# Linear attention and a routed expert layer on one core: the attention steps in another written order, with other tables of PSUM banks

## The chip, the cores and the metric

The kernel runs on one NeuronCore of a Trainium2 chip. Times are device microseconds of that core from launch to end; a kernel's time is the median of its runs. Lower is better. Five engines work side by side and each takes its own instructions strictly in order: TensorE (PE; its weight loads are PEld), VectorE (DVE), ScalarE (ACT), GpSimd (POOL) and the DMA-issuing queue of SyncE (SP).

## What is computed

```python
def phi(x):                                   # q, k, v: 8 batches, 8 heads, 576 tokens, 64 wide
    proj = einsum('bhsd,df->bhsf', x, w_phi)  # 128 features
    proj = proj - max(abs(proj), axis=-1)
    return concat([exp(proj), exp(-proj)])    # 256 features
kv  = einsum('bhsf,bhsd->bhfd', phi(k), v);   z = sum(phi(k), axis=2)
att = einsum('bhsf,bhfd->bhsd', phi(q), kv) / (einsum('bhsf,bhf->bhs', phi(q), z) + 1e-6)
x   = att as 4608 rows of 512
logits = x @ w_gate + modality_bias[modality_id];  e = argmax(logits);  gate = softmax(logits)[e]
out = gate * (relu(x @ w1[e]) @ w2[e])        # 8 experts, 512 -> 1024 -> 512
```

## The kernel before

Attention comes first. Its 64 (batch, head) pairs are worked in 16 groups of four, numbered 0 to 15. Each group is a set of small generators, one per kind of work, and every generator is cut into numbered steps; `K0.9` with step 2 is written K0.9.2 here. One step mostly holds work for one engine:

- K0, K1 (`k`, L469): 1 PE projects a half of the keys (16 matmul instructions, tile `pk`, one of the two large PSUM pairs); 2 DVE takes the largest absolute value (L480); 3 DVE subtracts it (L483), which is the last reader of the PSUM pair; 4 ACT makes both exponentials (L487).
- E (`e`, L490): 1 PE projects the last 64 tokens of keys and queries into two small banks; 2 ACT copies; 3 DVE maxima (L508); 4 ACT exponentials.
- Q0, Q1 (`q`, L517): 1 PE projects queries (`pq`); 2 ACT copies them to `d` (L527); 3 POOL finds the largest absolute value over the partitions (two PARTITION_ALL_REDUCE, L531); 4 DVE subtracts (L533); 5 ACT exponentials.
- V (`v`, L541): 1 and 2 PE multiply values with the features of K0 and of K1 (32 matmul instructions each, `kvT`), 3 PE adds the last tokens, 4 ACT copies.
- T (`t`, L564): 1 PE transposes the product, 2 ACT copies. Z (`z`, L591): 1 to 3 DVE add key features in place (L598), 4 PE sums them (`zp`), 5 ACT copies, 6 PE transposes, 7 DVE copies.
- N0, N1, D, L: numerators and denominators (`pn`, `pd`, `pl`), with copies out by ACT or DVE (for D of an odd group, the second step is the DVE operation at L652). XR, XA, XB, XL: transposes back to rows (`rp`, `xp`, `rl`), scaling on DVE (L693 to L708) and the store of the rows. R: the routing of two batches, with scatters by POOL. P: the early plan of which expert rows come first, ten steps of small DVE operations (L225 to L333). ML, RL: loads of row lists and expert weights.

At the end of attention the steps of the first expert slot are mixed in: W0 to W7 split weights, TU and TV transpose gathered rows, XS and XV split those (L856, L858), M0 to M3 are the first expert matmuls (L875), S0 and S1 the second (L892). After that the remaining expert slots run one behind the other.

The order of all 889 steps is written out by hand in `ORDER` (L1154), and inside `manual_schedule` every engine of SP, PE, ACT and DVE takes its instructions in just that order. POOL's reductions are chained in the same order (`Line`). PSUM has eight banks: the pool `pm` has four small ones and `pw` has two pairs. Which one a step's tile takes is read, one entry for each tile in order, from `PM_BANKS` (158 entries) and `PW_BANKS` (118 entries) at L1198. A step that takes a bank waits until the last reader of that bank's previous tile is done. When the last K, Q or E step has been written, `pw` is closed and its room goes to the experts (L1348); transposes after that use the whole array and a `pm` bank instead of two row halves and a `pw` pair.

Of the kernel before, what the change touches and what calls it, by code (L numbers as in the profile page):

```python
# [1151 lines left out]


ORDER = """  # L1154
    K0.0 E.0 Q1.0 E.0 K0.0 K0.0 K1.0 K0.0 E.0 V.0 Q1.0 K0.1 K1.0 K1.0 K0.1 Q0.0 E.0 K1.0 K0.1 Q0.0 K0.1 V.0 V.0 V.0
# [4 lines left out]
    Z.2 E.3 E.3 Q0.3 Q1.3 Q0.3 D.1 E.3 L.1 L.1 T.2 T.2 Z.2 L.1 D.1 K0.4 K1.4 K1.3 K0.4 K1.4 K0.4 Z.2 Q1.3 N0.2 E.3  # L1160
    Q1.3 K0.4 N1.2 K1.4 V.3 Z.2 N0.2 Z.2 Z.2 E.4 N1.2 Q0.3 Q0.3 XR.1 XB.1 XR.1 XB.1 V.3 V.3 XB.1 Q1.3 Z.3 Z.3 K1.4
    Q1.4 V.3 Z.3 Q0.3 E.4 E.4 Q1.4 Q0.4 Q0.4 D.2 D.2 L.2 T.3 T.3 CB.0 E.4 K0.5 K0.5 XA.1 XA.1 L.2 K0.5 Z.3 XA.1 V.4
    K1.5 K0.5 N1.3 L.2 V.4 Q1.4 Q1.4 V.4 Q0.4 K1.5 Z.3 K1.5 Q0.4 Q1.4 Z.3 Z.3 Q1.5 V.4 E.5 Q0.5 N1.3 L.3 Q0.4 D.3 E.5
    Z.4 Q0.5 Z.4 L.3 Q1.5 T.4 Z.4 K1.5 Q0.5 L.3 K0.6 N0.3 CB.0 T.4 D.3 N0.3 Z.4 Z.4 K0.6 E.5 K0.6 K0.6 N1.4 Q0.5 Z.4
    Z.4 K1.6 K1.6 N1.4 Q0.5 Q1.5 Q1.5 E.5 XL.3 XL.3 XL.3 V.5 Q1.5 V.5 V.5 XR.3 E.6 E.6 K1.6 XR.3 V.5 K0.7 E.6 K1.6 E.6
    K0.7 Z.5 XA.3 V.6 V.6 XA.3 XA.3 L.4 D.4 K0.7 Z.5 T.5 T.5 Q1.6 Q1.6 Q1.6 Q0.6 Q0.6 Z.5 V.6 K1.7 D.4 V.6 Z.6 Z.6
    XB.3 Z.5 N0.4 K1.7 L.4 L.4 K0.7 N0.4 Z.6 K1.7 N1.5 Z.5 Q1.6 N1.5 K1.7 N0.5 XB.3 XB.3 N0.5 Z.6 Z.6 R.3 Z.5 Z.5 Q0.6
    Q1.6 Q0.6 E.7 K0.8 K0.8 Z.6 Q0.6 E.7 Z.6 K0.8 E.7 E.7 V.7 V.7 Q1.7 Q1.7 Q0.7 Z.7 Q1.7 V.7 V.7 Z.7 Q0.7 L.5 T.6 L.5
    Z.7 T.6 K0.8 K1.8 T.7 L.5 Z.7 K1.8 T.7 Q0.7 Z.7 D.5 K1.8 K1.8 Q1.7 Q1.7 D.6 D.6 D.5 N1.6 Q0.7 N0.6 Z.7 N0.6 N1.6
    Z.7 XR.5 E.8 Q0.7 Q1.8 E.8 R.3 XR.5 R.3 Q1.8 K0.9 K0.9 E.8 E.8 K0.9 V.8 V.8 XA.5 XA.5 Q0.8 L.6 Q0.8 Z.8 XA.5 V.8  # L1170
    Q1.8 K0.9 Q1.8 XB.5 L.6 L.6 Q1.8 V.8 K1.9 N0.7 XB.5 K1.9 Q0.8 Q0.8 N0.7 N1.7 D.7 XB.5 N1.7 T.8 K1.9 Q0.8 E.9 Q0.9
    E.9 Z.8 T.8 E.9 Q0.9 Q0.9 R.3 E.9 K0.10 Z.8 K1.9 Q1.9 Q1.9 Z.8 Q1.9 L.7 R.3 K0.10 K0.10 D.7 N1.8 Z.8 Z.8 Z.8 K1.10
    L.7 L.7 XL.7 V.9 R.3 K0.10 R.3 Q0.9 K1.10 V.9 Q0.9 K1.10 K1.10 XL.7 XL.7 N0.8 Q1.9 N0.8 XR.7 XA.7 XR.7 XA.7 XA.7
    V.9 V.9 Z.9 Z.9 R.7 N1.8 D.8 T.9 E.10 T.9 D.8 Q1.9 E.10 K0.11 K0.11 E.10 Q0.10 Q0.10 R.7 Z.9 V.10 V.10 K0.11 E.10
    R.7 Z.9 V.10 K0.11 V.10 K1.11 K1.11 K1.11 Q1.10 Q1.10 L.8 N1.9 Q0.10 Q0.10 K1.11 Z.9 XB.7 XB.7 XB.7 Q1.10 Q0.10
    R.7 R.7 R.7 L.8 R.7 N0.9 T.10 N1.9 N0.9 T.10 Q1.10 Q1.10 L.8 Z.10 Z.10 Q0.11 E.11 E.11 Q0.11 Q0.11 V.11 E.11 V.11
    Z.9 Z.9 K0.12 Z.10 K0.12 Q1.11 E.11 V.11 V.11 CB.0 Z.10 K0.12 L.9 Z.10 Z.10 Q1.11 Z.10 Q1.11 K1.12 T.11 R.3 D.9
    L.9 L.9 K1.12 N1.10 K0.12 Q0.11 N1.10 T.11 K1.12 D.10 D.9 Q1.11 CB.0 R.3 XR.9 XR.9 Q0.11 XA.9 XA.9 Q1.11 N0.10
    E.12 XA.9 Z.11 N0.10 Q1.12 Q0.12 E.12 Q1.12 Z.11 Q0.12 E.12 E.12 Q1.12 L.10 D.10 XB.9 K0.13 L.10 N0.11 Q0.12 R.7
    K1.12 Z.11 Z.11 Z.11 XB.9 XB.9 N0.11 N1.11 K0.13 K0.13 R.7 R.7 Q1.12 Z.11 K1.13 N1.11 K1.13 V.12 V.12 L.10 K0.13  # L1180
    Z.11 Q1.12 L.11 K1.13 L.11 D.11 Q0.12 Z.12 Z.12 Q0.12 D.11 V.12 L.11 Z.12 Q0.13 E.13 XR.11 XR.11 V.12 E.13 Q0.13
    E.13 Q0.13 Z.12 K1.13 XL.11 E.13 XL.11 R.11 Q1.13 V.13 V.13 Q1.13 XA.11 XL.11 T.12 Q1.13 R.11 R.11 R.11 Q0.13
    XA.11 Z.12 V.13 T.12 V.13 XA.11 R.11 Z.12 N0.12 N1.12 Q0.13 N0.12 Z.12 Q1.14 R.11 R.11 Q1.13 Q0.14 E.14 Q1.13 E.14
    Q0.14 Q1.14 Q0.14 D.12 P.11 D.12 N1.12 P.11 P.11 Z.13 Z.13 Z.13 K0.14 K0.14 T.13 Q1.14 R.3 Z.13 Z.13 R.11 T.13
# [5 lines left out]
    T.15 Z.15 T.15 ML.11 ML.11 W1.15 TU.15 Z.15 W3.15 Z.15 W0.15 N1.15 W3.15 N1.15 W0.15 D.15 XS.15 XS.15 XS.15 XS.15  # L1190
    L.14 D.15 L.15 L.14 L.15 L.15 W4.15 W4.15 M1.15 M1.15 M1.15 W6.15 XL.15 W5.15 XR.15 XR.15 XL.15 R.15 W5.15 R.15
    TV.15 M0.15 R.15 M3.15 W7.15 M0.15 M0.15 M3.15 R.15 N0.14 M2.15 R.15 R.15 XV.15 R.15 W6.15 M3.15 M2.15 W7.15 N0.15
    XV.15 M2.15 X3.15 X3.15 R.15 R.15 R.15 XV.15 N0.15 XV.15 S0.15 S0.15 S1.15 S1.15 XL.15 XL.15 X0.15 X0.15 X1.15
    X1.15 X2.15 X2.15
# [237 lines left out]
```

## Time and profile before

| | us |
|---|---|
| median of 3 runs | 750.12 (749.88 to 751.48) |
| the profiled execution's own time | 751.13 |
| its span, first to last instruction | 749.2 |
| PE busy in the span | 726.9 |
| attention with its handover, up to the first expert matmul | about 290 |
| only experts, 290 to 700 | PE busy 408.9 of 410 |

The page's first part gives each engine's busy time, its table in 40 slices shows where that time lies, and the table by stretches repeats it for chosen windows together with the clock that TensorE was granted (1.00 is 2.4 GHz, 0.50 is 1.2 GHz). In the lists of instructions a row that ends in `[x <-engine tile]` says that the engine stood idle for x us before it, and what ended that.

### The profile page before, as it was taken

To read this page: it belongs to the slowest core of one execution; us is meant where nothing else is said; L and a number is where in the kernel's file an instruction comes from. 1 tells how busy PE (TensorE), PEld (TensorE's weight loads), DVE (VectorE), ACT (ScalarE), POOL (GpSimd) and SP (SyncE) were. 2 spreads that over 40 slices of the span, in tenths; PEclk is the share of its full clock that TensorE was granted. 3 is DMA by queue.
4 is the path that set the end of the run, shared out by engine and by line. 5 is a ranking of instruction groups with operands and counts; after the bars stand their busy time and mean duration, and the time that the engine had idled before them with its cause. 6 is when DMAs were issued, how large, how long until landed. Compare 5 with 4: busy or idle time off the path is not lost. (4 is left out here: it accounts for less than half of the span.)

```text
span 749.2 us, 19074 instructions
## 1 busy us (share of the span) xinstructions
PE 726.9 (97%) x7617; PEld 565.4 (75%) x7617; DVE 551.3 (74%) x832; ACT 446.9 (60%) x677; POOL 298.1 (40%) x200
## 2 busy tenths in 40 slices
...
GB/s 228 192 151 169 191 107 139 72 195 160 139 123 172 34 171 299 143 292 299 279 147 391 299 349 183 294 259 225 340 280 233 366 153 208 384 295 243 210 186 31
DMA packets 57111, 161.68 MB, mean 216 GB/s; under 512 B 21481, under 2 KB 24237, under 8 KB 44720
## 3 DMA queue, kind: packets, MB, share of 16 engines
...
q8 instruction: 65, 1.06, 0.6%
...
## 5 line engine op out<-in xcount | busy, mean ns | idle before, releaser
L838 ACT CAST h<-raw 128x1024 fp32r<-128x1024 f32 x148 | 149.7, 1050 | 99.5 <-PE p L892 47.9
L840 DVE TENSOR_TENSOR l<-raw,h 128x1024 fp32r<-128x1024 f32 x148 | 175.7, 1221 | 44.2 <-ACT h L838 31.3
L531 POOL PARTITION_ALL_REDUCE mq<-d x64 | 144.3, 2321 | 85.3 <-ACT d L527 50.0
L875 PE MATMUL p<-xh,h 128*128 128x256 f32 x576 | 164.2, 285 | 0.0
L875 PE MATMUL p<-xh,l 128*128 128x256 f32 x576 | 163.4, 284 | 0.0
L875 PE MATMUL p<-xl,h 128*128 128x256 f32 x576 | 163.2, 283 | 0.0
L796 POOL DMA_INDIRECT xg<-x,me x40 | 55.2, 1380 | 175.9 <-PE pt L848 86.4
L875 PEld LDWEIGHTS p<-xh,l 128*128 128x128 f32 x576 | 110.4, 192 | 2.0 <-issue 2.0
L875 PEld LDWEIGHTS p<-xh,h 128*128 128x128 f32 x576 | 110.4, 192 | 1.6 <-issue 1.2
L875 PEld LDWEIGHTS p<-xl,h 128*128 128x128 f32 x576 | 110.4, 192 | 0.5
L881 DVE SCALAR_TENSOR_TENSOR hl<-p,hh 128x512 fp32r<-128x512 f32 x72 | 49.5, 688 | 82.9 <-ACT hh L879 82.2
L879 ACT ACTIVATE hh<-p 128x512 fp32r<-128x512 f32 x72 | 42.8, 595 | 110.6 <-PE p L875 108.3
L892 PE MATMUL p<-h,hh 128*128 128x512 f32 x272 | 104.6, 395 | 0.0
L892 PE MATMUL p<-h,hl 128*128 128x512 f32 x272 | 103.4, 390 | 0.0
L892 PE MATMUL p<-l,hh 128*128 128x512 f32 x272 | 103.2, 390 | 0.0
L538 ACT ACTIVATE qp<-d 128x1152 f32<-128x1152 f32 x64 | 70.9, 1164 | 6.8 <-DVE d L533 6.6
...
L487 ACT ACTIVATE kp<-dk 128x1024 f32<-128x1024 f32 x64 | 64.4, 1060 | 10.4 <-DVE dk L483 9.0
L598 DVE TENSOR_TENSOR kp<-kp 128x1024 f32<-128x1024 f32 x48 | 62.9, 1335 | 0.2
L550 PE MATMUL kvT<-kp,va 128*32 128x256 f32 x1024 | 59.7, 381 | 0.9 <-ACT kp L487 0.8
L892 PEld LDWEIGHTS p<-h,hl 128*128 128x128 f32 x272 | 51.1, 188 | 10.9
L892 PEld LDWEIGHTS p<-l,hh 128*128 128x128 f32 x272 | 51.1, 188 | 10.3
...
## 6 DMA issues: line engine op xcount, KB each, us to landing
...
```

The costliest lines, as they stand in the source:

```text
L487: nc.scalar.activation(kp[:, :, :, s, :].rearrange("p t a f -> p a t f"), dk, AF.Exp, scale=sc)
L531: self.line(nc.gpsimd.partition_all_reduce(mq[:, a], d[:, a], P, bass_isa.ReduceOp.absmax))
L538: nc.scalar.activation(q["qp"][:, 2 * pr:2 * pr + 2, i, :], d, AF.Exp, scale=sc)
L550: nc.tensor.matmul(pt[pr][32 * c:32 * c + 32], va[:, pr, t, 32 * c:32 * c + 32], kp[:, pr * 4 + t, c // 2, :, :], start=t == 0, stop=False ...
L598: nc.vector.tensor_tensor(kv4[:, :, t], kv4[:, :, t], kv4[:, :, u], ALU.add)
L796: g = self.nc.gpsimd.indirect_dma_start(xg, None, self.x[:rows, :], IndirectOffsetOnAxis(ix.bitcast(U32), 0), bounds_check=rows - 1, oob_i ...
L838: nc.scalar.copy(h, r)
L840: nc.vector.tensor_tensor(l, r, h, ALU.subtract)
L875: nc.tensor.matmul(pp[:, j], a[:, cc, f], b[:, cc], start=i == 0, stop=i == 11)
L879: nc.scalar.activation(self.HH[:, sl], pp, AF.Relu)
L881: nc.vector.scalar_tensor_tensor(self.HL[:, sl], pp, 0.0, self.HH[:, sl], ALU.max, ALU.subtract)
L892: nc.tensor.matmul(pp, a[:, f, tk], b[:, f], start=i == 0, stop=i == 23)
```

## The change

`ORDER` is replaced by another order of the same 889 steps: every step occurs as often as before, and only the sequence differs. `PM_BANKS` and `PW_BANKS` are replaced too, with the same number of entries. Two conditions are added so that group 15's two attention transposes (T.15 and Z.15.6) take a `pm` bank and the whole array even where they stand before the end of `pw`, as T.15 does in the new order; before, they stood behind it and did so anyway. No instruction is added, removed or resized, on any engine.

```diff
     def turns_of(self, pm, name, n, blocks):
 
-        if self.pw:
+        if self.pw and not name.endswith(str(NQ - 1)):
...
-        if self.pw:
+        if self.pw and qi < NQ - 1:
             tp = self.turns_of(pm, f"zt{n}", 1, [zT])[:, :, 0]
         else:
             tp = pz[:, P:2 * P]
...
 ORDER = """
-    K0.0 E.0 Q1.0 E.0 K0.0 K0.0 K1.0 K0.0 E.0 V.0 Q1.0 K0.1 K1.0 K1.0 K0.1 Q0.0 E.0 K1.0 K0.1 Q0.0 K0.1 V.0 V.0 V.0
-    Q1.0 Q1.0 Q1.0 Q0.0 K1.1 E.1 K0.2 K1.1 K1.1 K1.1 Q1.1 Q0.0 Q0.0 E.1 Q1.1 Z.0 Z.0 Z.0 E.1 V.1 CB.0 K0.2 V.1 Q0.1
...
-    L.12 Q0.14 Q0.14 K0.15 XB.11 XB.11 E.15 V.14 V.14 V.14 K0.15 Q1.15 Q1.14 Q1.14 P.11 N1.13 Z.14 Z.14 N1.13 L.13
-    D.13 K0.15 E.15 Q1.15 T.14 Q1.15 P.11 P.11 P.11 RL0.15 L.13 T.14 Z.14 K1.15 D.13 Q0.15 N1.14 E.15 ML.11 ML.11 L.13
-    K0.15 K1.15 K1.15 Z.14 Q0.15 XR.13 XR.13 XA.13 XA.13 XA.13 E.15 K1.15 V.15 V.15 V.15 Z.14 Q1.15 Q1.15 XB.13 Q0.15
...
+    K0.0 E.0 E.0 K0.0 K0.0 Q1.0 Q1.0 K0.0 Q0.0 Q0.0 E.0 E.0 K1.0 K1.0 K1.0 K0.1 K0.1 K1.0 Q1.0 Q1.0 Q1.0 CB.0 K0.1
+    K0.1 K1.1 K1.1 V.0 V.0 Q1.1 E.1 V.0 Z.0 V.0 V.1 Q0.0 Q0.0 Q0.0 Z.0 K1.1 K0.2 Z.0 K0.2 E.1 Q1.1 CB.0 E.1 Z.0 K1.1
...
+    E.14 Q1.14 Z.13 Z.13 V.14 P.11 Z.13 K1.14 K1.14 CB.0 K0.15 Z.13 K1.14 Q1.14 T.13 D.12 D.13 V.14 Q0.14 K0.15 Q0.14
+    K0.15 D.13 V.14 T.13 K0.15 Q0.15 P.11 V.14 Q1.14 Z.14 P.11 P.11 P.11 P.11 Q1.14 E.15 E.15 Q1.15 N0.13 Z.14 Z.14
+    N1.13 N0.13 Q1.15 N1.13 R.11 R.11 L.13 Q0.15 R.11 E.15 E.15 Q1.15 P.11 P.11 T.14 T.14 K1.15 K1.15 Z.14 V.15 K1.15
+    N1.14 RL0.15 L.13 L.13 Z.14 Z.14 ML.11 K1.15 Q1.15 Q1.15 ML.11 XR.13 V.15 Z.14 XR.13 V.15 N1.14 Q0.15 Q0.15 XA.13
...
```

## Rows read from the trace of the kernel before

**Rows 1.** The page: the span, and busy time of each engine.

```profile
span 749.2 us, 19074 instructions
PE 726.9 (97%) x7617; PEld 565.4 (75%) x7617; DVE 551.3 (74%) x832; ACT 446.9 (60%) x677; POOL 298.1 (40%) x200
```

**Rows 2.** Stretches: window, length, busy PE, PEld, DVE, ACT, POOL; clock, DMA share, GB/s.

```profile
0.00:40.00 40.00, 34.10 (x431) 20.02 (x435) 33.80 (x63) 28.77 (x49) 20.45 (x18) 1.00 0.72 197
40.00:260.00 220.00, 216.92 (x3574) 126.17 (x3566) 202.82 (x306) 184.56 (x318) 146.81 (x76) 1.00 0.49 140
269.00:272.50 3.50, 3.50 (x48) 1.93 (x36) 2.41 (x3) 2.02 (x6) 3.50 (x2) 0.51 1.01 421
290.00:700.00 410.00, 408.88 (x2917) 367.64 (x2910) 264.60 (x400) 193.65 (x252) 103.36 (x87) 1.00 0.73 271
```

**Rows 3.** Instructions of PE in order: start, us, line, tile, count [idle before].

```profile
23.03 1.13 PE L523 MATMUL pq<-qt,wp 64*128 64x512 f32 x4 [1.43 <-DVE dk L483]
...
265.05 1.03 PE L523 MATMUL pq<-qt,wp 64*128 64x512 f32 x4
268.45 2.70 PE L627 MATMUL pn<-qp,kv 128*32 128x448 f32 x16 [2.38 <-DVE dn L652]
270.91 1.53 PE L606 MATMUL zp<-kp,ones 128*32 128x128 f32 x24
...
272.65 0.46 PE L578 MATMUL rp<-ident,dn 64*128 64x64 f32 x8
272.95 0.66 PE L578 MATMUL xp<-ident,xt 64*128 64x64 f32 x16
273.54 3.66 PE L550 MATMUL kvT<-kp,va 128*32 128x256 f32 x64
...
278.43 1.71 PE L627 MATMUL pn<-qp,kv 128*32 128x448 f32 x16
279.96 1.06 PE L627 MATMUL pl<-qp,kv 128*32 128x128 f32 x32
...
290.09 0.39 PE L875 MATMUL p<-xh,h 128*128 128x256 f32 x1
```

**Rows 4.** Instructions of DVE in order: the plan and its neighbours at 263 us.

```profile
262.90 0.20 DVE L308 TENSOR_REDUCE ote<-g3e 128x6 f32<-128x48 f32 x1
263.13 1.94 DVE L241 TENSOR_TENSOR ote<-ote,k256te 128x6 f32<-128x6 f32 x1
...
265.34 1.21 DVE L598 TENSOR_TENSOR kp<-kp 128x1024 f32<-128x1024 f32 x1
266.47 1.26 DVE L244 TENSOR_SCALAR k256tl<-kf 128x16 f32<-128x16 f32 x1
...
267.73 0.67 DVE L652 SCALAR_TENSOR_TENSOR dn<-pd,eps,dn 128x448 f32<-128x448 f32 x1
...
288.84 1.28 DVE L858 TENSOR_TENSOR xl<-pt,xh 128x512 fp32r<-128x512 f32 x2
```

**Rows 5.** Groups of instructions, 0 to 290 us: count | busy us, mean ns of one.

```profile
L487 ACT ACTIVATE kp<-dk 128x1024 f32<-128x1024 f32 x64 | 64.4, 1060 | 10.4 <-DVE dk L483 9.0 <-PE zp L606 1.4
L598 DVE TENSOR_TENSOR kp<-kp 128x1024 f32<-128x1024 f32 x48 | 62.9, 1335 | 0.2
L533 DVE TENSOR_TENSOR d<-d,mq 128x1152 f32<-128x1152 f32 x32 | 48.9, 1529 | 1.7 <-POOL mq L531 1.4
L483 DVE TENSOR_TENSOR dk<-pk,mk 128x1024 f32<-128x1024 f32 x32 | 39.0, 1219 | 2.9 <-ACT kp L487 1.7
L480 DVE TENSOR_REDUCE mk<-pk 128x8 f32<-128x1024 f32 x32 | 38.8, 1215 | 8.4 <-PE pk L477 8.3
L508 DVE TENSOR_REDUCE me<-pe 128x1 f32<-128x128 f32 x32 | 7.7, 282 | 1.5 <-ACT d L504 1.5
```

**Rows 6.** One line's instructions: shortest, median and longest, in ns.

```profile
L598 DVE TENSOR_TENSOR kp<-kp x48: 1211/1218/2556, 24.1 to 281.1; 128x1024 f32<-128x1024 f32 x48
L533 DVE TENSOR_TENSOR d<-d,mq x32: 1339/1354/2455, 18.3 to 277.0; 128x1152 f32<-128x1152 f32 x32
```

More of the change, by code (lines that the diff above doesn't have):

```diff
@@ L1154 @@
 ORDER = """
-    K0.0 E.0 Q1.0 E.0 K0.0 K0.0 K1.0 K0.0 E.0 V.0 Q1.0 K0.1 K1.0 K1.0 K0.1 Q0.0 E.0 K1.0 K0.1 Q0.0 K0.1 V.0 V.0 V.0
-    Q1.0 Q1.0 Q1.0 Q0.0 K1.1 E.1 K0.2 K1.1 K1.1 K1.1 Q1.1 Q0.0 Q0.0 E.1 Q1.1 Z.0 Z.0 Z.0 E.1 V.1 CB.0 K0.2 V.1 Q0.1
-    E.1 Q0.1 V.1 Z.1 V.1 E.2 K0.2 T.0 T.0 CB.0 Z.0 Z.0 CB.0 CB.0 N0.0 Z.0 K0.2 T.1 Q1.1 N0.0 N1.0 Q1.1 T.1 Z.0 L.0
-    Q0.2 Q1.1 N1.0 L.0 Z.1 Q0.1 Q0.1 Q0.1 Z.1 K1.2 E.2 L.0 K1.2 N1.1 Q0.2 E.2 E.2 K1.2 K1.2 V.2 K0.3 Q1.2 Q1.2 K0.3
-    K0.3 Z.1 N1.1 D.0 Z.1 K1.3 D.0 V.2 K0.3 Q0.2 Q0.2 Q1.2 K1.3 K1.3 N0.1 Q0.2 V.2 V.2 Z.1 Q1.2 Z.1 N0.1 Q1.3 Q1.2 Z.2
@@ L1160 @@
[L1160 to L1184, printed above, removed]
@@ L1185 @@
-    L.12 R.11 P.11 R.11 K0.14 K0.14 Z.13 Z.13 P.11 E.14 E.14 P.11 K1.14 XB.11 L.12 N0.13 K1.14 V.14 K1.14 N0.13 K1.14
-    L.12 Q0.14 Q0.14 K0.15 XB.11 XB.11 E.15 V.14 V.14 V.14 K0.15 Q1.15 Q1.14 Q1.14 P.11 N1.13 Z.14 Z.14 N1.13 L.13
-    D.13 K0.15 E.15 Q1.15 T.14 Q1.15 P.11 P.11 P.11 RL0.15 L.13 T.14 Z.14 K1.15 D.13 Q0.15 N1.14 E.15 ML.11 ML.11 L.13
-    K0.15 K1.15 K1.15 Z.14 Q0.15 XR.13 XR.13 XA.13 XA.13 XA.13 E.15 K1.15 V.15 V.15 V.15 Z.14 Q1.15 Q1.15 XB.13 Q0.15
-    V.15 Z.14 Q0.15 Z.14 Z.15 Z.15 N1.14 Z.15 N0.14 L.14 D.14 XB.13 Z.15 XB.13 Q0.15 RL1.15 W2.15 D.14 W1.15 W2.15
@@ L1190 @@
[L1190 to L1194, printed above, removed]
+    K0.0 E.0 E.0 K0.0 K0.0 Q1.0 Q1.0 K0.0 Q0.0 Q0.0 E.0 E.0 K1.0 K1.0 K1.0 K0.1 K0.1 K1.0 Q1.0 Q1.0 Q1.0 CB.0 K0.1
@@ new lines @@
+    K0.1 K1.1 K1.1 V.0 V.0 Q1.1 E.1 V.0 Z.0 V.0 V.1 Q0.0 Q0.0 Q0.0 Z.0 K1.1 K0.2 Z.0 K0.2 E.1 Q1.1 CB.0 E.1 Z.0 K1.1
+    Q1.1 Z.0 K0.2 Q0.1 Q0.1 V.1 Q0.1 T.0 E.1 K1.2 T.0 K0.2 Z.0 Z.0 Q1.1 V.1 K1.2 K1.2 V.1 Q1.1 N0.0 N0.0 N1.0 T.1 T.1
+    N1.0 E.2 Q0.1 Q0.1 Q0.2 Z.1 CB.0 Z.1 Z.1 E.2 E.2 Q1.2 L.0 N1.1 Q1.2 L.0 Q0.2 K1.3 E.2 Q1.2 K0.3 K1.3 K1.2 V.2 N1.1
+    Z.1 Z.1 K0.3 K0.3 K0.3 D.0 D.0 V.2 V.2 Z.1 Q1.2 K1.3 Q1.2 Z.1 Q0.2 L.0 Q0.3 Q0.2 V.2 Z.2 Z.2 Q1.3 E.3 Q0.2 E.3
+    Q1.3 Q0.3 Q1.3 D.1 D.1 L.1 N0.1 E.3 Z.2 E.3 K1.3 Q0.3 T.2 K0.4 K0.4 K0.4 Z.2 V.3 Z.2 T.2 V.3 V.3 L.1 L.1 Q1.3 K0.4
@@ new lines @@
+    N0.1 V.3 Q1.3 Z.2 Z.2 XR.1 E.4 XR.1 Q0.4 Q0.3 XB.1 XB.1 N0.2 N0.2 XB.1 Q0.3 N1.2 E.4 D.2 Q0.4 D.2 Z.3 Z.3 Z.3 K1.4
+    K1.4 Q1.4 L.2 Q1.4 E.4 K1.4 E.4 Q0.4 K1.4 K0.5 K0.5 XA.1 XA.1 Q0.4 K0.5 Z.3 N1.2 Q0.4 XA.1 V.4 V.4 L.2 Z.3 L.2 V.4
+    T.3 Q1.4 T.3 K1.5 CB.0 V.4 Q1.4 K0.5 Z.3 Q1.4 Z.3 E.5 K1.5 N1.3 N1.3 L.3 K1.5 L.3 CB.0 Z.4 Z.4 E.5 T.4 E.5 Q0.5
+    Z.4 Q0.5 T.4 D.3 E.5 K1.5 K0.6 Q0.5 Q1.5 N0.3 K0.6 L.3 K0.6 Q1.5 Z.4 Z.4 N0.4 Z.4 N0.3 K0.6 K1.6 D.3 CB.0 Q1.5
+    N0.4 V.5 V.5 Q0.5 K1.6 K1.6 Q0.5 V.5 Q1.5 V.5 XL.3 Z.4 E.6 Q1.5 E.6 XL.3 XR.3 XL.3 N1.4 T.5 XR.3 T.5 Q1.6 Q1.6
@@ new lines @@
+    Q1.6 Q0.6 Z.5 Z.5 Q0.6 L.4 XB.3 K0.7 E.6 E.6 K1.6 N1.4 V.6 Z.5 Z.5 Z.5 D.4 D.4 XB.3 XB.3 XA.3 L.4 K0.7 Q0.6 K0.7
+    Q1.6 K1.7 N0.5 K0.7 XA.3 XA.3 V.6 V.6 K1.7 Z.5 Q0.6 Q1.6 L.4 N0.5 K1.7 V.6 Q0.6 E.7 Z.5 R.3 Q0.7 Q1.7 N1.5 E.7
+    Q1.7 Q1.7 Z.6 Z.6 Z.6 N1.5 E.7 D.5 T.6 Q0.7 K0.8 K0.8 D.5 Q0.7 T.6 K1.8 K1.7 K0.8 E.7 L.5 Z.6 Z.6 V.7 L.5 K0.8
+    Q1.7 Q1.7 K1.8 K1.8 V.7 Z.7 N0.6 N0.6 V.7 V.7 L.5 XR.5 R.3 Z.6 Q0.7 Q0.7 N1.6 CB.0 Z.6 XR.5 Z.7 T.7 T.7 E.8 Q1.8
+    Q0.8 E.8 Q1.8 Q0.8 N1.7 N1.7 E.8 R.3 E.8 XB.5 Z.7 K1.8 K0.9 K0.9 R.3 L.6 XB.5 N1.6 Z.7 Z.7 D.6 D.6 XB.5 K0.9 XA.5
@@ new lines @@
+    Q0.8 Q0.8 K1.9 R.3 N0.7 L.6 Q1.8 XA.5 Q1.8 Q0.8 N0.7 L.6 V.8 K0.9 XA.5 V.8 K1.9 K1.9 Q1.8 V.8 V.8 Z.7 Z.7 E.9 Z.8
+    Q1.9 E.9 Q1.9 Q0.9 Q1.9 D.7 L.7 Q0.9 Z.8 E.9 T.8 K0.10 Z.8 E.9 Z.8 D.7 K1.9 V.9 L.7 T.8 N0.8 K0.10 K0.10 Q1.9 Z.8
+    Z.8 L.7 N0.8 XR.7 E.10 Z.8 XR.7 XA.7 XA.7 Q0.9 V.9 XA.7 Q0.9 Z.9 Q1.9 K0.10 V.9 Z.9 V.9 XL.7 XL.7 Q0.10 Q0.9 V.10
+    E.10 XL.7 Q0.10 N1.8 N1.8 Z.9 E.10 K1.10 K1.10 Q1.10 Q1.10 K1.10 D.8 E.10 T.9 R.7 K0.11 T.9 K0.11 K1.10 XB.7 XB.7
+    D.8 XB.7 R.3 K0.11 Q0.10 L.8 Z.9 Z.9 Q1.10 Q0.10 L.8 V.10 Z.9 K1.11 Z.10 V.10 L.8 K0.11 N0.9 V.10 N1.9 Q0.10 R.3
@@ new lines @@
+    Z.10 R.3 N0.9 Z.9 D.9 T.10 E.11 Q1.10 K1.11 K1.11 Q1.10 Q0.11 N1.9 E.11 Q0.11 Q0.11 R.7 Z.10 Z.10 D.9 Z.10 L.9 R.7
+    T.10 Z.10 E.11 Z.10 K1.11 Q1.11 Q1.11 L.9 R.7 K1.12 Q1.11 R.7 R.7 E.11 L.9 K0.12 K0.12 K0.12 N1.10 N1.10 K1.12
+    K0.12 D.10 D.10 Q0.11 Q0.11 Q1.11 V.11 V.11 V.11 K1.12 V.11 XR.9 XR.9 Q1.11 E.12 Z.11 Q1.12 E.12 XB.9 Z.11 XB.9
+    R.7 Q1.12 K1.12 L.10 XB.9 V.12 E.12 T.11 T.11 Z.11 K0.13 Q0.12 K0.13 K0.13 Q1.12 E.12 Q0.12 Z.11 V.12 Z.11 Q1.12
+    Q0.12 N0.10 N0.10 Z.11 K1.13 Z.11 K0.13 XA.9 V.12 L.10 V.12 Q1.12 Z.12 N1.11 K1.13 D.11 N0.11 R.3 R.3 L.10 Q0.12
@@ new lines @@
+    Q0.12 N1.11 K1.13 L.11 D.11 N0.11 XA.9 L.11 XA.9 T.12 T.12 E.13 Z.12 Z.12 L.11 E.13 Q1.13 XL.11 Z.12 Q1.13 R.7
+    E.13 E.13 R.7 XL.11 XR.11 XL.11 XA.11 N1.12 Z.12 K1.13 XR.11 XA.11 XA.11 Q1.13 R.11 R.11 Q0.13 R.11 K0.14 Q0.13
+    N1.12 R.11 Q1.13 Q1.13 K0.14 R.7 Q0.13 R.11 K0.14 K0.14 Z.12 V.13 Z.12 R.11 R.11 V.13 N0.12 Z.13 V.13 V.13 Q0.13
+    XB.11 XB.11 Q0.14 N0.12 E.14 Q0.13 E.14 Q0.14 Q0.14 P.11 Z.13 Z.13 L.12 D.12 K1.14 XB.11 L.12 E.14 L.12 P.11 Q1.14
+    E.14 Q1.14 Z.13 Z.13 V.14 P.11 Z.13 K1.14 K1.14 CB.0 K0.15 Z.13 K1.14 Q1.14 T.13 D.12 D.13 V.14 Q0.14 K0.15 Q0.14
```

14 lines of the change are left out of this document (10 added, 4 removed).

## The prediction

> **What bounds the kernel now.** I read the page first, then the table by stretches, then the waits, then PE's and DVE's instructions where PE stands still. The page [rows 1] says PE is busy for 97% of the span, but the stretches decide [rows 2]. From 290 to 700 us there is only expert work, and PE idles 1.1 us of 410. The new order ends a little behind 290 us, so what it can do is move the moment at which PE gets into that unbroken run. Before 260 us PE is also nearly full: from 40 to 260 it idles 220 - 216.92 = 3.1 us. DVE is close behind, busy 202.8 of those 220 us. PE's idle time lies at the two ends: 5.9 us in the first 40 us, where the queues fill, and a wait of 2.38 us that ends at 268.45 [rows 3], followed by 3.5 us at half clock (granted 0.51, so 1.2 GHz). The change has no new instruction, so its price is the difference of the waits at three places: head, middle and end of attention.
>
> **The end of attention.** Before the change, PE finishes the queries of group 15 at 265.05 + 1.03 = 266.08 and then stands for 2.38 us [rows 3]. The next step, N1.14.1, takes the small bank of D.13, whose last reader is the DVE operation at L652. That starts at 267.73 [rows 4], because DVE takes its steps as written: P.11's last steps, with one add that took 1.94 us for 6 elements, the add Z.14.3 at 265.34, then a constant of the later plan for 1.26 us, then D.13.2. PE starts again at 268.45, and 5.09 us later, at 273.54, it begins V.15.1. In between lie N1.14.1 (279.96 - 278.43 = 1.53 us at full clock), Z.14.4 (272.65 - 270.91 = 1.74 us, mostly at half clock, so 0.87), XR.13.1 (0.30) and XA.13.1 (272.95 to 273.54, 0.55 at full clock): 3.25 us of work [rows 3]. So 2.38 + 5.09 - 3.25 = 4.2 us are lost here.
>
> In the new order D.13.2 stands directly behind K0.15.3, ahead of P.11's fourth to tenth steps, and no PE step meets that wait. I compared what stands ahead. The PE steps written before Z.14.4 in the new order are the very same set as those before N1.14.1 in the old one, so PE should come to Z.14.4 at 266.08. On DVE the steps up to Z.14.3 are the same but for three: P.11.9 and P.11.10 now come later (262.90 to 265.34, 2.4 us) and D.13.2 is already done (0.6). So Z.14.3 ends at 265.34 + 1.21 - 2.4 + 0.6 = 264.7, and PE need not wait for it.
>
> What is late next is V.15.2, which reads the exponentials of K1.15. PE does Z.14.4 (0.87), V.15.1 (half of 3.66, 1.8), N1.14.1 (1.53), Z.14.6 (0.1) and XR.13.1 (0.30) and is there at 270.7 [rows 3]. DVE does, from 264.7, E.15.3 (2 x 0.28), the two plan steps with the later plan's constants, and K1.15.2 and .3 (1.22 + 1.22); then ACT makes two exponentials (2 x 1.06) [rows 5]. The plan part is uncertain: 2.4 + 1.26 = 3.7 us if each small operation is as slow as in this trace, about 1.2 if all six take the 0.20 of an undisturbed one [rows 4]; I take the middle, 2.4. The exponentials then end at 264.7 + 0.6 + 2.4 + 2.4 + 2.1 = 272.2, and PE waits 1.5 us (between 0.3 and 2.8). V.15.2 starts at 272.2, when the old order had 1.34 us to go to V.15.1, and PE has done 1.8 + 0.1 - 0.55 = 1.35 us more. That is 2.7 us ahead, with ends at 1.4 and 3.9.
>
> From there to the first expert matmul the gain can shrink. It started at 290.09, and the DVE part of the row split that feeds M1 ended at 290.12 [rows 3, 4], so the chain of weight and row splits on ACT and DVE was as late as PE. The new order writes N0.15.1 (1.53) and a first transpose (0.1) ahead of M1.15. If that chain comes no earlier, PE still has 1.6 us more behind it when it gets there. I take 2.2 us between 1.6 and 2.7.
>
> PE's clock halved after the 2.38 us of idleness, and stayed at 1.00 after 1.43 us at 23 us [rows 2, 3]. The Trainium skill, "TensorE: Matmul & The Clock Gate", section "What's actually happening", has an idle array fall to 1.2 GHz; the trace agrees, 0.51 behind that wait. By it a V.15.2 that waits as long as N1.14 did would pay the half clock once more, which the middle value of 1.5 us would not.
>
> **The head.** No stretch of the trace shows the new head. I counted, over the first 60 or so steps of each order, the places where the PE work written between a step and the step that takes its bank or its result is shorter than that step's own chain (for K 1.22 + 1.22 on DVE, and 2.1 more on ACT if V wants the result [rows 5]). The old order has eight, which lack 7.7 us; the new has six, which lack 5.7. One is new: K1.1 takes K1.0's pair with one 0.9 us step in between, and lacks 1.8. That would be a gain of 2.0. But the queues speak against it: the new order puts Q0.0, K1.0, K0.1 and K1.1 on PE ahead of V.0, so all DVE and ACT steps of four K halves stand together, and V.1 waits for V.0's copy behind a pair of exponentials (2.1). Following the four queues with these durations to the first K step of group 3, I come out 0.7 us behind. I take a loss of 0.4, between a gain of 2.0 and a loss of 2.1.
>
> **The middle.** From about step 100 to the end the same count gives six places lacking 1.4 us before and seven lacking 1.6 after: a draw, 0. As a gain it is bounded by PE's idle 3.1 us [rows 2]. As a loss it is bounded by one wait like that of N1.14 with its half clock (4.2 us) or by slower DVE work (below): 5. DMA issues move with their steps, loads of group n + 2 still follow the fifth projection of group n, and the DMA share of 0.49 [rows 2] leaves room; I cost them at nothing, covered by the two groups of lead, and a load that came late would show as PE waiting on `kt` or `qt`.
>
> **Sum.** -2.2 (end) + 0.4 (head) + 0 (middle) = -1.8 us. Against the profiled execution, 751.13 with its span of 749.2 and 1.9 around it, that is 749.3; that execution is 1.0 above the median of 750.12, so the median should be 748.3.
>
> **Rivals.** *The gain is hidden.* The splits ahead of M1 keep the experts where they were but for the 1.6 us, and the head costs 1.1 or more: -0.5 us or less, 749.6. For it: 290.09 and 290.12 lie together [rows 3, 4]. Against it: DVE itself comes out of the plan earlier. *Slower: DVE work under the reductions.* Two kinds of DVE operation take longer at times: the adds of Z, 1211 ns at best and up to 2556, and the subtractions of Q, 1339 up to 2455 [rows 6]. Over the means that is 48 x 0.124 + 32 x 0.190 = 12.0 us [rows 5, 6], and in the trace every long one overlaps a reduction on POOL. The place is the middle. If the new order lays ten more of them under a reduction at 0.7 us each, DVE has 7 us more, and as it has only 17 us of 220 idle I would let two thirds reach PE: 748.3 + 4.7 = 753.0. It decides from about five more on (2.3 us, which eats the gain and the head's loss). Against it: adds written between a copy into `d` and its subtraction, where a reduction can run, number 25 of 48 before and 24 after, and subtractions written so are 16 of 32 in both; but only 7 of those 25 adds were hit, so the count leaves room. The Trainium skill, "GPSIMD Engine Reference", section "1. Specifications", says that GpSimd's way to SBUF is shared with VectorE for instructions with two SBUF inputs, which both kinds are; the trace agrees, 2556 ns beside 1211. *Nothing comes of the reordering*: the engines run in the new order but end level, 750.1; the middle's draw speaks for it, the wait at 268 us against it.
>
> **How the numbers follow.** Forecast 46%; hidden gain 17% and level 7%, together 24% within 0.2%; DVE under reductions 22%, and the half clock falling once more at V.15.2 or elsewhere with a loss in the head 8%. About 0.2%, 1.5 us, is what a measurement of this kernel can tell from no change, so faster means under 748.6. Faster 0.46, same 0.24, slower 0.30. The range reaches down to 743.5 (end 3.9 and head 2.0 as gains, and a part of the middle's 3.1, leaves 1 in 10) and up to 754.0 (the 753.0 of the slower rival and a head at its worse end). Both signs hold much of the chance; the forecast's own range is 746 to 750.
>
> **What would show it.** In the changed profile: no wait of N1.14 or of another PE step for `dn` at L652 beyond 0.5 us, and PEclk 1.00 throughout attention; a wait of 0.3 to 2.8 us at the second half of `kvT` of group 15 on `kp` L487; the first L875 at about 288 us, with a `pn` more done ahead of it; PE busy from 40 to 260 us within 1 us of 216.9; means of L598 and L533 within 0.05 us of 1.335 and 1.529. I am wrong if the first L875 comes behind 290, or if it comes early and the experts behind it stand still.

## The result

The changed kernel takes 743.54 us (742.11 to 745.47) beside 749.95 us (748.90 to 751.48) for the kernel before, a ratio of 0.9914 with a 95% interval of 0.9892 to 0.9936. That is 6.4 us faster; 1.8 were forecast. The profiled execution of after has a span of 741.5 us against 749.2 [rows 1]. The lines of its page that answer to these:

```profile
span 741.5 us, 19062 instructions
PE 724.4 (98%) x7617; PEld 565.0 (76%) x7617; DVE 539.3 (73%) x832; ACT 446.4 (60%) x677; POOL 294.1 (40%) x200
```

PE does the same work in 2.5 us less, in part because it no longer falls to half clock at 269 us. DVE has the same 832 instructions and is busy for 12 us less. The stretches of after, with the columns of [rows 2]:

```profile
0.00:40.00 40.00, 34.69 (x431) 20.47 (x435) 31.84 (x62) 30.41 (x51) 19.79 (x18) 1.00 0.78 212
40.00:260.00 220.00, 219.04 (x3618) 127.64 (x3614) 199.82 (x313) 187.27 (x324) 147.25 (x79) 1.00 0.49 138
269.00:272.50 3.50, 3.50 (x72) 2.21 (x68) 3.07 (x4) 3.41 (x7) 0.69 (x1) 1.00 0.45 119
290.00:700.00 410.00, 408.82 (x2909) 369.12 (x2908) 263.13 (x398) 193.68 (x253) 102.05 (x88) 1.00 0.72 269
```

From 40 to 260 us PE idles 1.0 us instead of 3.1, and between 269 and 272.5 the clock is 1.00 instead of 0.51. Inside the experts nothing changed. The end of attention on PE in after, in the form of [rows 3]:

```profile
262.51 0.86 PE L606 MATMUL zp<-kp,ones 128*32 128x128 f32 x24
...
263.41 1.91 PE L550 MATMUL kvT<-kp,va 128*32 128x256 f32 x32
265.14 1.69 PE L627 MATMUL pn<-qp,kv 128*32 128x448 f32 x16
...
268.26 1.93 PE L550 MATMUL kvT<-kp,va 128*32 128x256 f32 x32 [0.98 <-ACT kp L487]
...
279.44 1.25 PE L848 MATMUL pt<-ident,xg 128*128 128x128 f32 x8
...
284.17 1.71 PE L627 MATMUL pn<-qp,kv 128*32 128x448 f32 x16
285.81 0.33 PE L588 MATMUL rl<-ident,dn 128*128 128x128 f32 x1
285.89 0.37 PE L875 MATMUL p<-xh,h 128*128 128x256 f32 x1
```

Z.14.4 starts at 262.51 (270.91 before), N1.14.1 at 265.14 with no wait (268.45 after 2.38 us of it), and V.15.2 waits 0.98 us for the exponentials. The first L875 comes at 285.89 instead of 290.09, and a `pn` and a transpose stand ahead of it.

To see where PE gains, I laid the PE sequences over each other by work done: every step counts with its shortest duration in the traces compared, and the table tells how much earlier a kernel has done so many us of work than the kernel before, in us (a plus is later). The last row is the 97th matmul of L892, in the second expert slot, at 355.57 us in the kernel before; from there on the lead of after stays within 0.05 us. The span of after is 7.7 us shorter; the other 1.4 us lie behind PE's last matmul, where the program takes 7.6 to 9.9 us in these traces.

| PE's work done | after | e1 | e2 | e3 | e4 | e12 |
|---|---|---|---|---|---|---|
| first K step (6.02 us before) | -0.36 | -0.54 | -0.54 | -0.54 | -0.54 | -0.54 |
| 30 us (45.5) | -1.06 | -0.57 | -0.54 | -1.06 | -0.75 | -1.46 |
| 140 us (164.0) | -1.62 | -0.56 | -0.54 | -1.61 | +0.09 | -2.01 |
| 210 us (241.8) | -2.42 | -0.55 | -0.55 | -2.44 | +0.11 | -2.78 |
| 230 us (264.4) | -3.81 | -0.54 | +0.92 | -1.84 | +0.12 | +1.19 |
| 240 us (279.2) | -6.58 | -2.78 | -2.30 | -4.62 | 0.00 | -0.75 |
| 97th L892 | -6.26 | -0.15 | -1.86 | -4.63 | -0.01 | -1.03 |

The first row is no effect of the order: the first loads landed that much earlier in those executions. For after the lead of 6.26 us is then 0.36 from the start, 0.70 in the head, 2.75 in the middle, 2.77 at the end of attention, less 0.32 in the handover.

The weighing has an error of some tenths of a us. It falls away at the places where both kernels have done just the same matmuls. There after is 1.39 us ahead at 49.0 us of the kernel before, 1.47 at 162.3, 2.64 at 227.6 and 6.57 at 278.4. Ahead of N1.14 before and of Z.14.4 in after it is 3.5 (PE would be free at 266.0, had it not to wait, and starts at 262.5). By these places the head is worth 1.0, the middle 2.1 and the end 3.1 us.

### The profile page after: what moved, and what is told of

It reads as the page before. It is cut to its first block, busy times and chain, and to the rows that moved or that the text cites. A ratio compares the mean times of both kernels' runs of the same rounds, so it can differ in the third digit from the quotient of the medians.

```text
span 741.5 us, 19062 instructions
## 1 busy us (share of the span) xinstructions
PE 724.4 (98%) x7617; PEld 565.0 (76%) x7617; DVE 539.3 (73%) x832; ACT 446.4 (60%) x677; POOL 294.1 (40%) x200
## 5 line engine op out<-in xcount | busy, mean ns | idle before, releaser
L875 PE MATMUL p<-xh,h 128*128 128x256 f32 x576 | 164.2, 285 | 1.2 <-DVE hl L881 1.2
L875 PE MATMUL p<-xh,l 128*128 128x256 f32 x576 | 163.3, 284 | 0.0
L875 PE MATMUL p<-xl,h 128*128 128x256 f32 x576 | 163.1, 283 | 0.0
L875 PEld LDWEIGHTS p<-xh,h 128*128 128x128 f32 x576 | 110.4, 192 | 2.8 <-DVE hl L881 1.4
L875 PEld LDWEIGHTS p<-xh,l 128*128 128x128 f32 x576 | 110.3, 192 | 2.0 <-issue 2.0
L875 PEld LDWEIGHTS p<-xl,h 128*128 128x128 f32 x576 | 110.4, 192 | 0.4
L892 PE MATMUL p<-h,hh 128*128 128x512 f32 x272 | 104.6, 395 | 0.0
L892 PE MATMUL p<-h,hl 128*128 128x512 f32 x272 | 103.4, 390 | 0.0
L892 PE MATMUL p<-l,hh 128*128 128x512 f32 x272 | 103.2, 390 | 0.0
L598 DVE TENSOR_TENSOR kp<-kp 128x1024 f32<-128x1024 f32 x48 | 59.9, 1265 | 0.2
L892 PEld LDWEIGHTS p<-h,hl 128*128 128x128 f32 x272 | 51.0, 188 | 10.8
L892 PEld LDWEIGHTS p<-l,hh 128*128 128x128 f32 x272 | 51.2, 188 | 10.3
```

The costliest lines, as they stand in the source:

```text
L875: nc.tensor.matmul(pp[:, j], a[:, cc, f], b[:, cc], start=i == 0, stop=i == 11)
L892: nc.tensor.matmul(pp, a[:, f, tk], b[:, f], start=i == 0, stop=i == 23)
```

## The experiments

Seven kernels are mixtures of the two orders, with banks given out anew where the mixture needs it; in four the order stands and the work of DVE or POOL is changed; one is the changed kernel itself. The mixtures carry the change's two added conditions too. e1 to e4 and e12 ran where the kernel before takes 749.6 to 750.0 us.

**e1: D.13.2 early, and nothing else.** The order of before with one step moved:

```diff
-... P.11.9 P.11.10 ... D.13.2
+... D.13.2 P.11.9 P.11.10 ...
```

> The order of before with one step moved: D.13.2 (the DVE operation at L652) goes ahead of P.11.9, P.11.10 and Z.14.3. Nothing is left out. Theory: the wait of 2.38 us at N1.14.1 is DVE's queue, so this one step takes it and the half clock behind it away. PE is then at V.15.1 about 4 us earlier, but V.15.2 and the row splits come late next, as in the new order; 2.0 to 3.5 us of 749.95 are gained: 746.5 to 748.0, PEclk 1.00 through attention. Rival: the lead of the new order comes from DVE being ahead through the whole middle, and the step's place alone only moves the wait to another PE step of group 14 or 15: 749.5 to 750.5, and the half clock stays.

Measured: 750.11 us, ratio 1.0002 (0.9992 to 1.0011). The time is the rival's. The wait at N1.14 is gone and PE gains 2.2 us between 230 and 240 us of its work, as the table shows. It then loses 3.5 us up to the first L875, which comes 0.74 us later than before. The rows of PE in e1:

```profile
265.46 1.71 PE L627 MATMUL pn<-qp,kv 128*32 128x448 f32 x16
...
269.87 0.46 PE L578 MATMUL rp<-ident,dn 64*128 64x64 f32 x8 [1.82 <-DVE dk L483]
...
281.76 0.27 PE L848 MATMUL pt<-ident,xg 128*128 128x128 f32 x1
283.73 1.67 PE L848 MATMUL pt<-ident,xg 128*128 128x128 f32 x7 [1.69 <-DMA xg<-x,me]
290.83 0.39 PE L875 MATMUL p<-xh,h 128*128 128x256 f32 x1
```

Of the old wait of 2.38 us, 1.82 come back two steps later, where XR.13 waits for K1.15's subtraction. The clock stays at 1.00 behind that, so that most of the 2.2 us is the half clock that doesn't follow. PE comes to TU.15 at 281.76 and stands until the gathered rows arrive, and the clock halves once more (the stretch from 283.9 to 287.3 has 0.50). POOL issues the gathers; its rows in before, e1 and after:

```profile
263.81 8.99 POOL L531 PARTITION_ALL_REDUCE mq<-d  x4
275.34 1.05 POOL L796 DMA_INDIRECT xg<-x,me  x1 [2.54 <-DMA me<-lst]
276.70 1.28 POOL L796 DMA_INDIRECT xg<-x,me  x1 [0.31 <-issue]
```

```profile
263.26 9.00 POOL L531 PARTITION_ALL_REDUCE mq<-d  x4
276.24 1.88 POOL L796 DMA_INDIRECT xg<-x,me  x1 [3.98 <-DMA x<-xs]
278.43 2.04 POOL L796 DMA_INDIRECT xg<-x,me  x1 [0.31 <-issue]
```

```profile
260.22 9.47 POOL L531 PARTITION_ALL_REDUCE mq<-d  x4
272.89 1.39 POOL L796 DMA_INDIRECT xg<-x,me  x1 [3.20 <-DMA me<-lst]
274.59 1.00 POOL L796 DMA_INDIRECT xg<-x,me  x1 [0.31 <-issue]
```

The gathers need the plan's list and the end of the last reductions. In e1 the last reduction ends 0.5 us earlier than before, but the gathers start 0.9 and 1.7 us later. For the first one the profile names a store of rows (`x<-xs`). By the semaphores in the trace that store landed at 275.86, when POOL's wait was over (275.47); what came late was the list, whose first load landed at 275.15, against 274.24 before. So in this execution the step that PE gained ends in a wait for rows that came later than before, and of that delay no run tells how much belongs to the order. In after the last reduction ends 3.1 us earlier, the gathers are 2.5 and 2.1 us earlier, TU at 279.44 doesn't wait, and the gain passes.

**e2: the old order, then the new one.** Before's order up to the step ahead of P.11.4, then the new one's:

```diff
-ORDER = before
+ORDER = before[: P.11.4] + (the steps left, in the order of after)
```

> The order of before up to P.11.4 (about 248 us), then the steps that are left in the order of after, each tile in the bank that its own order gave it. Nothing is left out. Theory (three separate places add up): the end of attention alone is worth what after's trace shows between the same PE work at about 250 and 277 us, 2.5 to 3.5 us: 746.5 to 747.5. Rival (the gain hangs on the whole order): with the old order's DVE lag the new end waits at V.15.2 instead, 749 to 750.5.

Measured: 749.49 us, 0.9995 (0.9984 to 1.0007). The time is the rival's, though V.15.2 waits only 0.69 us. The seam costs 1.5 us (the table's step from 210 to 230; 1.04 of it is a wait ahead of a projection of keys at 253.79 for which the profile names nothing), the end of attention gains 3.2, and 1.9 of PE's lead stays in the profiled execution, 1.3 without its start. The median moves by 0.5, within the interval. So the new tail does its step here too, and by itself, with its seam, it is worth less than can be measured.

**e3: the new order, then the old one.** After's order up to the step ahead of P.11.8, so with D.13.2 already early, then before's:

```diff
-ORDER = after
+ORDER = after[: P.11.8] + (the steps left, in the order of before)
```

> The order of after up to P.11.8, then the steps that are left in the order of before. Nothing is left out. Theory of separate places: head and middle are worth 3 to 4 us, and the old end gives its wait and its half clock back: 746.0 to 747.0, with a wait of some 2 us on `dn` at N1.14.1 or near it if D.13.2 stands behind the plan again. Rival: since DVE comes to the plan earlier, the old end waits for nothing either, 743 to 744.5.

Measured: 743.68 us, 0.9919 (0.9907 to 0.9932): the whole gain, as the rival had it. N1.14 doesn't wait and the clock stays at 1.00. Rows of PE in e3:

```profile
265.51 1.71 PE L627 MATMUL pn<-qp,kv 128*32 128x448 f32 x16
...
268.03 0.46 PE L578 MATMUL rp<-ident,dn 64*128 64x64 f32 x8
```

N1.14.1 starts at 265.51 with the same matmuls done as before, where PE would have been free at 266.0. That is 0.5 us earlier, and 0.54 of it is the start: the lead of head and middle is lost at this seam. The 4.6 us of the table arise behind it. The wait of N1.14 and the half clock are gone, as in e1, but XR.13 at 268.03 and TU wait for nothing: K1.15's subtraction starts at 266.89 (268.50 in e1), and the gathers at 271.99 and 273.72. So what the new head and middle give in e3 is no lead of PE but chains on DVE and POOL that are earlier. The profiled execution took 744.80 us, 1.1 above the median. The rows of DVE in e3 that answer to [rows 4]:

```profile
259.17 0.20 DVE L308 TENSOR_REDUCE ote<-g3e 128x6 f32<-128x48 f32 x1
259.41 0.17 DVE L241 TENSOR_TENSOR ote<-ote,k256te 128x6 f32<-128x6 f32 x1
259.61 0.17 DVE L319 CAST oite<-ote 128x12 int32<-128x12 f32 x1
...
260.98 0.17 DVE L244 TENSOR_SCALAR k256tl<-kf 128x16 f32<-128x16 f32 x1
```

The plan's small operations stand ahead of the last reductions, which begin at 263.32 here, and take 0.17 to 0.24 us each. Before, the same add took 1.94 us and the constant 1.26 [rows 4].

**e4: the new head, then the old order.** After's order up to the step ahead of K0.3.1:

```diff
-ORDER = before
+ORDER = after[: K0.3.1] + (the steps left, in the order of before)
```

> The order of after up to K0.3.1 (the first 97 steps, some 45 us), then the steps that are left in the order of before. Nothing is left out. Theory: the head is worth the 0.7 us that lie between the two traces at the same PE work, less than is measured: 749.0 to 750.0, and the wait at N1.14.1 with its half clock stays. Rival: the head decides how far DVE runs ahead of PE from there on, and a third or more of the whole gain comes with it: 747.8 or less.

Measured: 749.68 us, 0.9998 (0.9989 to 1.0007), as the theory had it. The lead of the head is lost before 140 us of work. The kernel also says something on DVE. Its groups, as in [rows 5]:

```profile
L598 DVE TENSOR_TENSOR kp<-kp 128x1024 f32<-128x1024 f32 x48 | 61.5, 1305 | 0.2
L533 DVE TENSOR_TENSOR d<-d,mq 128x1152 f32<-128x1152 f32 x32 | 47.1, 1474 | 2.2 <-POOL mq L531 2.1
```

They are 3.2 us shorter than before (62.9 + 48.9 - 61.5 - 47.1), nearly all of it ahead of 60 us, and this brought nothing.

**e12: the new order to V.13.3, then the old one.** As e3, with the cut 58 steps earlier, so that D.13.2 is late again:

```diff
-ORDER = after
+ORDER = after[: V.13.3] + (the steps left, in the order of before)
```

> The new order up to the step ahead of V.13.3 (683 of 889 steps, about 205 us of PE's work), and then the steps that are left in the order of before: D.13.2 stands late again, behind P.11.10, as in the kernel before. Theory 'the middle carries it' (with the middle, the plan's last steps get done on DVE ahead of the last reductions, so neither N1.14's wait nor the gather is late): within 0.2% of the kernel that keeps the new order up to P.11.8, that is a ratio of 0.990 to 0.994 to before, no wait of N1.14 over 0.5 us, the operation at L241 that took 1.94 us before under 0.7, clock 1.00. Theory 'the middle is needed but not enough; D.13.2 must stand early too': N1.14 waits 1.5 us or more, the half clock follows, and the ratio is 0.995 to 0.998. Theory 'neither': 1.000.

Measured: 749.17 us, 0.9998 (0.9985 to 1.0012), and none of the three held as written. PE is 2.8 us ahead at 210 us of work; by 230 it has lost that and 1.2 more, most of it at the seam. Its rows in e12:

```profile
243.37 0.80 PE L497 MATMUL pe<-wp,kt 64*128 64x128 f32 x4 [2.65 <-ACT xt L644]
...
268.69 1.71 PE L627 MATMUL pn<-qp,kv 128*32 128x448 f32 x16 [1.42 <-DVE dn L652]
```

E.14.1 takes a small bank whose last reader, the copy at L644, is late in this mixture, and the clock is 0.50 from 243.0 to 246.4. So e12 doesn't tell whether the middle alone would do. It does show that a lead of 2.8 us at group 13 is lost by one late bank, and that with D.13.2 late N1.14 still waits 1.42 us.

The other seven ran on another chip, on which the kernel before takes 760 us, and they tell less.

**e11: the changed kernel again.**

> The changed kernel once more, beside the two above on the same chip: every theory expects a ratio of 0.991 to before.

Measured: 757.21 us (752.6 to 761.26) beside 759.98, 0.9961 (0.9937 to 0.9985). The gain is 2.8 us here, not 6.4. Up to 140 us of PE's work the trace runs as that of after to 0.2 us; then PE stands still in the middle of small matmuls of one step. Rows of PE in e11:

```profile
226.45 0.30 PE L627 MATMUL pl<-qp,kv 128*32 128x128 f32 x2 [1.03 <-issue]
227.87 1.12 PE L627 MATMUL pl<-qp,kv 128*32 128x128 f32 x4 [1.12 <-issue]
```

"issue" means that the profile shows nothing that PE waited for. The trace of after has no such row between 100 and 290 us; in e11 they come to 4.2 us, the clock is 0.50 from 227.3 to 234.1, and the first L875 is at 296.64. Their cause is open. They fall at other places in every kernel, so that differences of a few us between kernels on this chip can't be put down to the orders.

**e7 and e8: the orders cut in the middle.** The new order up to V.8.4 and then the old (e7), and the old up to Q0.8.3 and then the new (e8).

```diff
+e7: ORDER = after[: V.8.4] + (the steps left, in the order of before)
+e8: ORDER = before[: Q0.8.3] + (the steps left, in the order of after)
```

> The new order up to the step ahead of V.8.4 (about 135 us of PE's work), and then the steps that are left in the order of before. Theory 'the middle's gain lies behind group 8', where DVE is busy for 103.4 of 110 us in the old order: no gain, 749 to 750.5, with PE idle from 150 to 260 us for 2 us or more. Theory 'it grows evenly over the middle': 746 to 747.5.

> The order of before up to the step ahead of Q0.8.3 (about 130 us of PE's work), and then the steps that are left in the new order. Theory 'the middle's gain lies behind group 8': nearly the whole gain, 743.5 to 745. Theory 'it grows evenly over the middle': 746 to 747.5.

Measured, beside 760.20: e7 759.02, 0.9995 (0.9978 to 1.0011), and e8 762.64, 1.0043 (1.0023 to 1.0063). In e7 the new order up to group 8 shows no gain, as in e4. e8 begins with a wait of 2.71 us of E.9.1 for the copy at L644, the same kind of seam as in e12, so it doesn't test where the gain lies and met neither theory; with the standstills of this chip, e7 doesn't settle it either.

**e5 and e6: half of the reductions left out**, in the old and in the new order.

```diff
-        for a in range(2):
-            self.line(nc.gpsimd.partition_all_reduce(mq[:, a], d[:, a], P, ...))
+        self.line(nc.gpsimd.partition_all_reduce(mq[:, 0], d[:, 0], P, ...))
-        nc.vector.tensor_tensor(d, d, mq, ALU.subtract)
+        nc.vector.tensor_tensor(d, d, mq[:, 0:1].to_broadcast([P, 2, S]), ALU.subtract)
```

> The order of before with its own bank table, but one reduction on POOL (L531) for each pair of heads in place of two: the second head's queries use the first head's maximum, so half of the reductions are left out and the output changes. The tokens fall to the experts as before, so the expert work is the same. Theory 'DVE under reductions' (the middle's gain of 3 to 4 us comes from DVE operations that are lengthened less: 48 x 0.070 + 32 x 0.063 = 5.4 us less DVE work in the new order): the lengthening goes down by about half in this kernel, the means of L598 and L533 fall below 1.30 and 1.45 us, PE's idle time from 150 to 260 us falls from 2.4 to about 1.2 us, the first L875 comes 2 us or more before 290.1, and the time is 746 to 748. Theory 'order alone' (the middle's gain lies in which steps stand between a bank's release and its next use, whatever DVE's pace): the time stays within 1 us of 749.9 and PE idles as before.

> The order of after with its own bank table, and the same half of the reductions left out as in the kernel above (output changed, expert work the same). Theory 'DVE under reductions': the two orders come closer, the difference falls from 6.4 us to 3 to 4.5, with this kernel at 742 to 743.5. Theory 'order alone': the difference to the kernel above stays at 6 us or more.

Measured, beside 760.20: e5 756.74, 0.9947 (0.9930 to 0.9965); e6 751.10, 0.9892 (0.9865 to 0.9920). Fewer reductions help both orders, by 3.5 us the old one, so they do cost time. In e5 the means of the two operations fall to 1.278 and 1.440 us, and the gain of 3.5 is what "DVE under reductions" expected, not "order alone" (within 1 us). The difference of the orders is 5.6 us, between the 3 to 4.5 of the one theory and the 6 or more of the other, and the two intervals leave about 2.5 us either way. So the pair doesn't decide between them; with all reductions the difference is 2.8 on this chip (760.0 less 757.2).

**e9 and e10: four adds less, four adds more.** In groups 8 to 11 the third add of Z is left out in the old order (e9), or done twice in the new one (e10).

```diff
+e9:            if (t, u) != (0, 2) or qi not in (8, 9, 10, 11):
+e10:           for _ in range(2 if (t, u) == (0, 2) and qi in (8, 9, 10, 11) else 1):
                 nc.vector.tensor_tensor(kv4[:, :, t], kv4[:, :, t], kv4[:, :, u], ALU.add)
```

> The order and the bank tables of before, but of the 48 adds of Z (L598, 1.22 us at best) the third of groups 8 to 11 is left out: four adds, 4.9 to 5.3 us less work for DVE between about 150 and 225 us, as much as the new order saved through shorter ones (5.4 us). Denominators change, and so does the output. Theory 'DVE is late at the end of attention, and both the waits from 150 us on and the wait of N1.14 come from that': they go without any change of order, PE idles under 1.5 us from 150 to 260 us (2.4 before), N1.14 waits under 0.5 us, the clock stays at 1.00, the plan and the gathers come about 3 us earlier, and the time is 743.5 to 746. Theory 'order alone' (the waits come from where D.13.2 and the banks stand): the wait of 2.4 us at N1.14 remains, 749 to 751.

> The new order with its own bank tables, and the same four adds done twice (groups 8 to 11, the third add), so DVE has 4.9 to 5.3 us more to do, which gives back what the new order saved; the output changes. Theory 'DVE is late at the end': most of the gain goes, 747.5 to 750, with PE idle from 150 to 260 us up by 1.5 us or more, and V.15.2's wait of 1.0 us grown to 3 us or more. Theory 'order alone': 743 to 745, with the waits of after.

Measured: 773.49 and 774.11 us beside 759.98 (1.0182 and 1.0191). I hadn't reckoned that other denominators send tokens to other experts: from the first L875 to PE's last matmul e9 takes 467.5 us and e10 460.4, against 450.1 in e11. Up to the first L875, e9 comes at 296.78 and e10 at 300.45, against 296.64 of e11; there is no trace of the kernel before on this chip. In e10 PE waits four times for the adds of Z, 3.8 us in all, from 40 to 300 us, so extra DVE work there does reach PE, but what the orders owe to DVE isn't settled by this pair.

## Why the prediction was right, and where it was off

The direction was right and the range held, but by luck: 743.54 lies 0.04 us above its lower end of 743.5, and outside the forecast's own 746 to 750. Of the 6.4 us, 1.8 were forecast. The point was 4.8 us too high; the middle carries about half of that, and the head 1.1 to 1.4.

*The end of attention, -2.2: right in size.* PE gains 2.77 us there, where 2.7 were worked out, and keeps 2.45 after the handover, against 2.2 (3.1 and 2.8 by the places of equal work). V.15.2 was to start at 272.2 after 1.5 us of waiting; it starts at 268.26 after 0.98, and 272.2 less the 3.5 us by which PE is earlier from Z.14.4 on is 268.7. The clock stayed at 1.00; that a wait of 1.5 us would not halve it rested on a single row of 1.43, and the waits of the last section show that the length alone is no ground for it. But the reason was only half right. Moving D.13.2 alone (e1) gains 2.2 us on PE and brings nothing: the next chain on DVE takes most of the wait back at XR.13, and TU the rest. The rival "the gain is hidden" is what happened in e1, at another place than I named: not the row split ahead of M1 but the gather by POOL, which waits for the plan's list and the reductions. The gain counts in after since this chain is earlier there too. I had costed the steps that PE and DVE go past and not this chain, which also sets when TU can start.

*The middle, 0: the mis-sized term.* It is -2.75 by the table and -2.1 by the places of equal work, within the bound of 3.1 that I gave as a gain from PE's idle time. The count of places that lack cover gave a draw, because it took median durations; the waits of before come from single places. Those between 180 and 250 us in before:

```profile
197.53 0.86 PE L606 MATMUL zp<-kp,ones 128*32 128x128 f32 x24 [0.29 <-DVE kp L598]
...
200.63 0.28 PE L578 MATMUL zt<-ident,zT 64*128 64x64 f32 x2 [0.71 <-DVE dk L483]
...
211.32 1.13 PE L523 MATMUL pq<-qt,wp 64*128 64x512 f32 x4 [0.47 <-DVE xs L708]
...
245.24 1.16 PE L477 MATMUL pk<-wp,kt 64*128 64x128 f32 x16 [0.62 <-ACT d L527]
...
246.80 0.86 PE L606 MATMUL zp<-kp,ones 128*32 128x128 f32 x24 [0.16 <-DVE kp L598]
```

They are 2.25 us, and after has a single one in that stretch, of 0.17:

```profile
228.63 0.71 PE L578 MATMUL xp<-ident,xt 64*128 64x64 f32 x16 [0.17 <-DVE xs_l L708]
```

These five rows were to be had before the forecast. Each could have been followed to the steps that stand around it in the new order; the count over all steps hid them. What in the new order took these waits away isn't shown: other steps between, or DVE's shorter operations.

I also took the three terms as a sum, and they aren't. e1 and e4 hold one part each and gain nothing, and e3, whose PE comes to N1.14 with no lead in the trace, gains all behind it, because the other chains there are earlier. A term that is in time by itself and waits for a late chain elsewhere has to be worked out together with what makes that chain earlier.

*The head, +0.4: -0.70 at PE by the table (-1.0 by equal work), and worth nothing alone* (e4 loses it again by 140 us of work). The places that came out 0.7 behind by following the queues were too pessimistic; the bounds of 2.0 and 2.1 held.

*The slower rival went the other way.* The means of L598 and L533 in after, with the columns of [rows 5]:

```profile
L598 DVE TENSOR_TENSOR kp<-kp 128x1024 f32<-128x1024 f32 x48 | 59.9, 1265 | 0.2
L533 DVE TENSOR_TENSOR d<-d,mq 128x1152 f32<-128x1152 f32 x32 | 46.8, 1466 | 0.4 <-POOL mq L531 0.4
```

They moved by 0.070 and 0.063 us, out of the 0.05 that I allowed, and down: 5.1 us of busy time less (111.8 against 106.7). e4 shows that 3.2 us of that, early in attention, reach nobody. I had let two thirds of a change reach PE; where it lies decides. Whether it matters near the end isn't shown. The plan's operations are short in e3, but in after they lie beside a reduction and are long, and both kernels take the same time. Those of after:

```profile
261.02 0.63 DVE L241 TENSOR_TENSOR ote<-ote,k256te 128x6 f32<-128x6 f32 x1
261.69 0.82 DVE L319 CAST oite<-ote 128x12 int32<-128x12 f32 x1
...
261.92 0.61 DVE L244 TENSOR_SCALAR k256tl<-kf 128x16 f32<-128x16 f32 x1
```

*Signs that I named.* The wait of N1.14, the clock, the wait at V.15.2 and the `pn` ahead of L875 came as said. The first L875 came at 285.89, not at about 288, and another step did wait for `dn` at L652 beyond 0.5 us, `rp` at 165.31 for 0.67. PE's busy time from 40 to 260 us (219.04, not within 1 of 216.92) and the two means did not come as said, and both pointed at the middle.

What stays open: whether the middle without an early D.13.2 would do (e12's seam hides it), what took the waits of the middle away (e5, e6, e9 and e10 don't settle it), and why the gain is only 2.8 us on the other chip.
